# Row maxima of an attention kernel: turned through TensorE and ScalarE, or by VectorE's 32x32 exchange

## The chip, the cores and the metric

The kernel runs on one core of a Trainium2 chip. The metric is the device time of one execution in microseconds, lower being better. The median of three runs of the kernel before is 1864.71 us (1864.58 to 1864.8).

## What is computed

Two attention blocks over the same shapes (one batch, sequence S = 2048, width D = 640, 32 heads of width 20) are computed and their outputs are put side by side. Block A looks at a window of 8 keys with a dilation of 2. Block B is full attention, and the change lies in it:

```python
qkv = (x @ wqkv).reshape(B, S, 3, H, Dh).transpose(2, 0, 3, 1, 4)
q, k, v = qkv[0], qkv[1], qkv[2]
scores = jnp.einsum("bhqd,bhkd->bhqk", q, k) * (Dh ** -0.5)
p = _softmax(scores, axis=-1)
o = jnp.einsum("bhqk,bhkd->bhqd", p, v)
return o.transpose(0, 2, 1, 3).reshape(B, S, D) @ wo
```

All is in float32.

## The kernel before

**Stages.** First come the projections of A (queries, keys and values written to DRAM as rows), then the queries and keys of B (lines 492 to 529), then the values of B (lines 730 to 761), and then the main loop over B's attention (lines 791 to 836), with a short end that projects the last outputs. Block A's windowed attention is done almost wholly by GpSimd, a unit of work at a time (`a_attention`, lines 370 to 393), beside the main loop and the stages just ahead of it.

**Tiling of B.** The 32 heads are taken in 8 groups of 4, the 2048 queries in 4 blocks of 512. One group with one block of queries is a unit `u`; there are 32. A unit has 16 steps of 128 keys each, so the main loop has 512 steps. Step `i` does four things:

- `b_qk(i)`, lines 644 to 661: TensorE multiplies 128 keys by 512 queries for the 4 heads (62 contracted rows for each), into banks of PSUM called `ps_st`, and ScalarE takes the exponential into `e`.
- `b_pv(i - 2)`, lines 663 to 687: TensorE multiplies the exponentials by the values. Every second step ScalarE copies the sum out (`braw`, `more`) and GpSimd adds it up (line 683).
- `b_max(i + 24)`, lines 584 to 605: TensorE multiplies queries by keys once more with queries on the partitions (60 contracted rows), into the double tiles `ps_mx`, of which there are two. VectorE reduces each of them (128x1024 to 128x2) to the largest score, two reductions in a step. They are written into `m4`, which the profile shows as `mx`.
- pieces of other work: output groups, loads, GpSimd's units of block A.

For units 27 to 29, `b_both` (lines 607 to 639) does the first and the third of these in another order.

**What the change touches.** The largest score of every query is subtracted inside the score product itself: a query tile `bq` has two rows (60 and 61 of its 62) that hold the largest score as a sum of a high and a low part, and the matching rows of the key tile hold -1. The maxima are found with queries on partitions but have to lie along a row. `max_rows` (lines 535 to 555) does this once for each unit, 32 times in all:

- VectorE reduces `m4` to `m1`, 128 partitions by 16 (two halves of the contracted rows by two heads by four blocks of 128 queries).
- `turn` (lines 540 to 547) takes a bank of `ps_st`. TensorE turns `m1` into it (16x128), ScalarE copies it as float32r into `mt[:, 0]` (the high part; `mt` is `mtr` in the profile), VectorE subtracts that from the bank and writes the low part into `mt[:, 1]`, and the bank is given back.
- one step later SyncE's queue writes `mt` to DRAM, `md` (`mdr` in the profile), as 32 runs of 512 bytes.
- another step later `load` (lines 549 to 552) reads two pieces of `md` into the rows of `bq`.

**What sets the order.** The order of each engine's work is written out by hand. Every engine takes its instructions in the order of the program (`InOrder`, lines 48 to 56). `after(n, f)` runs `f` at the n-th next `tick()`, and the main loop ticks once at the head of a step. `b_max` of the last step of unit u runs in loop step 16u - 9; `odd(1)` puts the reduction to `m1` into step 16u - 7. `turn` is put on the list `rows` at the head of step 16u - 5, and it is taken off that list in the same step (line 821) just behind the first pair of score products; in units 29 to 31, whose maxima come from `b_both`, behind all of `b_both` (line 808). In the values' stage it is taken off at lines 756 and 757. The transfer to `md` is issued in step 16u - 4, the two loads in step 16u - 3, and the first score product that reads them is in step 16u.

Banks: `bank()` hands out four tiles `ps_st` in turn (lines 88 to 100), so that each use of one waits for the use four places before.

Of the kernel before, what the change touches and what calls it, by code (L numbers as in the profile page):

```python
# [8 lines left out]
F32 = mybir.dt.float32  # L9
F32R = mybir.dt.float32r  # L10
AF = mybir.ActivationFunctionType
ALU = mybir.AluOpType
# [47 lines left out]
def attention_pair(ctx, tc, xa, wqk_a, wv_a, wo_a, xb, wqk_b, wv_b, wo_b, oa, ob):  # L60
# [3 lines left out]
    sb = ctx.enter_context(tc.tile_pool(name="sb", bufs=1))  # L64
    ps = ctx.enter_context(tc.tile_pool(name="ps", bufs=1, space=PS))
    dr = ctx.enter_context(tc.tile_pool(name="dr", bufs=1, space=bass.MemoryType.DRAM))
    pe, dve, act, gp, sp = (InOrder(tc, e) for e in (nc.tensor, nc.vector, nc.scalar, nc.gpsimd, nc.sync))
# [5 lines left out]
    def after(n, fn, *args):  # L73
        due.setdefault(now[0] + n, []).append((fn, args))
# [3 lines left out]
    def odd(n):  # L78

        return n if loop[0] is None else n + (now[0] + n - loop[0] + 1) % 2  # L80

    def tick():
        now[0] += 1
        for fn, args in due.pop(now[0], ()):
            fn(*args)
# [5 lines left out]
    def bank():  # L91

        n = free.pop(0)
        t = ps.tile([128, 512], F32, tag=f"st{n}", bufs=1, name="ps_st")
        taken[id(t)] = (n, t)
        return t

    def give(t):

        free.append(taken.pop(id(t))[0])  # L100
# [45 lines left out]
    def chunk(t, xi, k):  # L146
        return t[k // (KC - 1)][:, xi, k % (KC - 1)]

    def x_pieces(x, n, second=None):

        t = columns(n)
        src = x[:, n * 512:(n + 1) * 512].rearrange("(k p) c -> p k c", p=128)

        def piece(a, b):
            u = t[a // (KC - 1)]
            m = a % (KC - 1)
            split(u[:, 0, m:m + b - a], u[:, 1, m:m + b - a], src[:, a:b], "p", second)
        return t, [lambda a=a, b=b: piece(a, b) for a, b in PAIRS]
# [58 lines left out]
    def rows15(p, o, W):  # L217

        for k in range(KC):
            for i, (wi, xi) in enumerate(PASSES):  # L220
                pe.matmul(p[:, :320], o(xi, k), W[wi][:, k], start=(k == 0 and i == 0), stop=(k == KC - 1 and i == 2))
# [40 lines left out]
    t, more = x_pieces(xa, 1)  # L262
# [6 lines left out]
    for n in (2, 3):  # L269
        t, more = x_pieces(xa, n)  # L270
        XA.append(t)
        loads += more
    ident = const.tile([128, 128], F32, name="ident")
# [149 lines left out]
    for n in range(NA):  # L423
        nxt = None
        for t in range(NT):
            if n == 0 and t < 4:
                p = first[t]
            else:
                p = next(banks)
# [51 lines left out]
    def v_piece(g, b0, b1):  # L481

        sp.dma_start(stacks[g][2][:, b0:b1], vb_d[b0 * 128:b1 * 128, g * GH * VC:g * GH * VC + VG]
                     .rearrange("(b p) c -> p b c", p=128))
# [8 lines left out]
    for m in range(0, 10, 2):  # L493
        nxt = []
        for n in range(4):
            for j in range(2):
                p = next(banks)
# [4 lines left out]
                c = MS[m + j]  # L502
# [27 lines left out]
    tick()  # L530


    rows = []

    def max_rows(m4, m1, q, qc):

        mt = sb.tile([16, 2, 128], F32R, tag="mtr", bufs=2, name="mtr")
        md = dr.tile([2, GH * 512], F32, tag="mdr", bufs=4, name="mdr")

        def turn():  # L540
            p = bank()
            pe.transpose(p[:16, :128], m1, ident)
            act.copy(mt[:, 0], p[:16, :128])
            dve.tensor_tensor(mt[:, 1], p[:16, :128], mt[:, 0].bitcast(F32), ALU.subtract)
            give(p)
            after(1, sp.dma_start, md.rearrange("t (j c) -> j t c", c=128), mt.bitcast(F32))
            after(2, load)

        def load():
            for r in range(2):  # L550
                sp.dma_start(q[r * HALF + BS:r * HALF + BM, qc].bitcast(F32),
                             md[:, r * 1024:(r + 1) * 1024].rearrange("t (p c) -> t p c", p=2))
        t = odd(1)
        after(t, dve.tensor_reduce, m1, m4.rearrange("p r a c -> p (r a) c"), AX.X, ALU.max)
        after(t + 2, rows.append, turn)

    def normalize(raw, g, c0, t, then):

# [25 lines left out]
    def b_max(i):  # L584

        u, sub = divmod(i, NKB)
        g, qc = divmod(u, NQC)
        q, k, v = stacks[g]
        if sub == 0:
            mxt[u] = (sb.tile([128, 2, 8, 4], F32, tag="mx4", bufs=2, name="mx4"),  # L590
                      sb.tile([128, 16], F32, tag="mx1", bufs=2, name="mx1"))
        m4, m1 = mxt[u]
        pq, ch = divmod(sub, 2)
        pl, qb = divmod(pq, 4)
        for c in (2 * ch, 2 * ch + 1):
            p = wide()
            for r in range(2):
                rows = slice(r * HALF, r * HALF + BS)
                pe.matmul(p[:, r], q[rows, qc, pl, qb * 128:qb * 128 + 128],
                          k[rows, pl, c * 512:(c + 1) * 512], start=True, stop=True)  # L600
            dve.tensor_reduce(m4[:, :, pq, c], p, AX.X, ALU.max)
            if c % 2 == 0:
                yield
        if sub == NKB - 1:
            max_rows(m4, m1, q, qc)

    def b_both(i):
# [30 lines left out]
        if sub == NKB - 1:  # L638
            max_rows(m4, m1, q1, qc1)
# [90 lines left out]
    for n in (2, 3, 0, 1):  # L730
        for half in range(2):
            for s in range(4 * n, 4 * n + 4):
                p = bank()
                rows15(p, lambda xi, k: chunk(XB[n], xi, k)[:, s % 4 * 128:s % 4 * 128 + 128], WV[half])
                ve = ones[s % 4]
                act.copy(ve[:, :16 * VC].rearrange("p (h c) -> p h c", c=VC)[:, :, :DH],
                         p[:, :320].rearrange("p (h d) -> p h d", d=DH))
                give(p)
                c = 16 * VC + 11 * half
                after(1, sp.dma_start, vb_d[s * 128:(s + 1) * 128, half * 16 * VC:half * 16 * VC + c], ve[:, :c])  # L740
                tick()
                groups += 1
                if q_loads:
                    for _ in range(4):
                        q_loads.pop(0)()
                if groups == 1:
                    wait[0] = 5
                if groups in (8, 16):
                    XB[groups // 8 - 1], more = x_pieces(xb, groups // 8 - 1, gp)
                    for fn in more:  # L750
                        fn()
                if groups > 8:
                    for i in islice(steps, 1):
                        for _ in b_max(i):
                            pass
                    if rows:
                        rows.pop(0)()
                if groups > 16 and groups % 3 == 0 and groups != 21:
                    next(a_work, None)
                if groups in (26, 28):  # L760
                    v_piece(0, *((0, 4) if groups == 26 else (8, 16)))
# [29 lines left out]
    for i in range(NS + LAG):  # L791
        g, sub = divmod(i, NQC * NKB)
        if sub == 16 and g + 1 < NG:
            k_loads, q_loads = b_pieces(g + 1)
            for n, fn in enumerate(k_loads + q_loads + [lambda g=g + 1: v_piece(g, 0, NKB)]):
                after(1 + n, fn)
        if i in (NS - 56, NS - 40):
            out_first((i - NS + 56) // NKB)
        tick()
        if loads and i % 2:  # L800
            loads.pop(0)()
        if i % 14 in (1, 5, 7, 11) and next(a_work, 0) == 0:
            for d in done_a:
                d[0] -= 1
        if i // NKB in ALONE and i + LEAD < NS:
            b_both(i)
            if rows and i % 2:
                rows.pop(0)()
            b_pv(i - LAG)
            if fill and i % 2 == 0:  # L810
                fill.pop(0)()
            elif i % 6 == 4 and not out_piece() and len(UNITS) == next_a[0] and not WO_b:
                for h in range(2):
                    w, more = wide_pieces(wo_b[h], gp)
                    WO_b.append(w)
                    loads += more
            continue
        qk = b_qk(i) if i < NS else iter(())
        next(qk, None)
        if rows and i % 2:  # L820
            rows.pop(0)()
        if i + LEAD >= NS:
            next(qk, None)
        if i >= LAG:
            b_pv(i - LAG)
        next(qk, None)
        mx = b_max(i + LEAD) if i + LEAD < NS else iter(())
        next(mx, None)
        if fill and i % 2 == 0:
            fill.pop(0)()  # L830
        elif i % 6 == 4 and not out_piece() and len(UNITS) == next_a[0] and not WO_b:
            for h in range(2):
                w, more = wide_pieces(wo_b[h], gp)
                WO_b.append(w)
                loads += more
        next(mx, None)
# [57 lines left out]
```

## Time and profile before

| | us |
|---|---|
| median of three runs | 1864.71 |
| the profiled execution, device time | 1864.39 |
| its span, first to last instruction | 1862.2 |
| busy: TensorE | 1818.1 |
| busy: ScalarE | 1374.9 |
| busy: VectorE | 1321.9 |
| busy: GpSimd | 1198.5 |

The profile is one execution, taken by the hardware profiler. PE is TensorE, PEld its loading of weights, DVE VectorE, ACT ScalarE, POOL GpSimd and SP SyncE, whose queue issues the transfers. All the program's instructions are issued by one helper, so that every row carries line 56, and a group is told by its tiles: output, an arrow, inputs. In a group's row stand the count, the busy time in us with the mean of one in ns, and behind the bar the idle time of the engine just before, with what ended it. In a row of the timeline stand the start and the length in us, the engine, the instruction, the tiles, the shapes, how many were merged, and in brackets the idle time ahead of it. The granted clock of TensorE was 0.998 over the span.

### The profile page before, as it was taken

The page shows a single profiled execution, that of the slowest core. Times are in us where ns is not written, and L with a number is a line of the kernel's source. Part 1 is how long each engine was busy: PE and PEld are TensorE (multiplying, and loading weights), DVE is VectorE, ACT ScalarE, POOL GpSimd, SP SyncE. Part 2 cuts the span into 40 slices and gives each one's busy share as a digit, 9 for nine tenths or more (in the row PEclk, how much of TensorE's full clock was granted, in tenths as well). Part 3 has the DMA queues.
Part 4 walks back from the last instruction along what each step waited for, and adds up shares of the span by engine and source line. Part 5 has one row for each costly group of instructions (what it writes and reads, how often), then busy time and mean ns, then how long its engine had stood idle before and what let it go on. Part 6 is the DMA issues. An engine that isn't in the chain of part 4 may idle for free.

```text
span 1862.2 us, 30622 instructions
## 1 busy us (share of the span) xinstructions
PE 1818.1 (98%) x11323; PEld 977.7 (52%) x11323; DVE 1321.9 (71%) x1286; ACT 1374.9 (74%) x2669; POOL 1198.5 (64%) x998
## 2 busy tenths in 40 slices
PE   9999999999999999999999999999999999999999
PEld 8888888885443433434434334343343344333558
DVE  3000332278889899898898998989989989999400
ACT  4222322224889899898898998989989988999882
POOL 0000075048989898898888988989889762557232
PEclk9999999999999999999999999999999999999999
DMA  6333686755542254345234432642452332111023
GB/s 222 113 95 115 206 291 234 229 156 172 135 132 95 96 158 141 97 113 153 89 103 133 137 98 89 165 137 75 129 162 86 99 75 61 54 31 49 29 67 111
DMA packets 144110, 229.74 MB, mean 123 GB/s; under 512 B 43100, under 2 KB 74460, under 8 KB 142968
## 3 DMA queue, kind: packets, MB, share of 16 engines
q1 hardware_dynamic: 143384, 227.13, 39.7%
q8 instruction: 89, 1.46, 0.3%
q10 hardware_dynamic: 576, 0.66, 0.1%
q14 instruction: 61, 0.50, 0.1%
HBM read 168.05 MB, written 59.67 MB: 122 GB/s over the span
## 4 chain that ended last, share of the span: by engine, by line
PE 64%; DVE 26%; ACT 6%; issue 2%; POOL 1%; POOLq 0%; ACTq 0%
PE ps_st L56 45%; DVE mx L56 25%; PE ps_mx L56 20%; ACT e L56 4%; ACT more L56 1%; POOL akv L56 1%; DVE am L56 0%; POOL braw L56 0%; DVE aot L56 0%; ACT aot L56 0%; POOL ao L56 0%; DVE sm L56 0%; ACT braw L56 0%; POOL am L56 0%; ACT ro L56 0%
## 5 line engine op out<-in xcount | busy, mean ns | idle before, releaser
L56 DVE TENSOR_REDUCE mx<-ps_mx 128x2 f32<-128x1024 f32 x1024 | 1201.3, 1221 | 143.6 <-PE ps_mx L56 136.8
L56 ACT ACTIVATE e<-ps_st 128x512 f32<-128x512 f32 x2000 | 1063.8, 615 | 50.9 <-PE ps_st L56 23.1
L56 PE MATMUL ps_st<-e,vb 128*32 128x512 f32 x4096 | 546.4, 606 | 1.0 <-ACT e L56 0.6
L56 PE MATMUL ps_st<-bq,bk 62*128 62x512 f32 x2000 | 491.2, 453 | 0.3
L56 PEld LDWEIGHTS ps_st<-bq,bk 62*128 62x128 f32 x2000 | 256.5, 184 | 439.0 <-ACT e L56 406.9
L56 POOL TENSOR_TENSOR braw<-braw,more 128x512 f32<-128x512 f32 x248 | 318.9, 1286 | 250.6 <-ACT more L56 247.8
L56 PE MATMUL ps_mx<-bk,bq 60*128 60x512 f32 x2048 | 442.7, 443 | 32.5 <-DVE mx L56 18.2
L56 POOL TENSOR_TENSOR akv<-akv,aq 128x1280 f32<-128x1280 f32 x64 | 188.3, 2943 | 236.7 <-DMA akv<-ka_d 236.7
L56 PEld LDWEIGHTS ps_mx<-bk,bq 60*128 60x128 f32 x2048 | 205.2, 185 | 180.8 <-DVE mx L56 168.5
L56 POOL TENSOR_TENSOR akv<-akv 128x640 f32<-128x640 f32 (+3 forms) x304 | 281.8, 927 | 23.8
L56 ACT COPY ro<-ps_st 128x320 f32<-128x320 f32 (+1 forms) x92 | 43.6, 474 | 159.3 <-PE ps_st L56 114.5
L56 PEld LDWEIGHTS ps_st<-e,vb 128*32 128x32 f32 x4096 | 80.9, 108 | 151.5 <-ACT e L56 87.0
L56 ACT COPY more<-ps_st 128x512 f32<-128x512 f32 x248 | 149.6, 603 | 11.6 <-PE ps_st L56 5.4
L56 POOL TENSOR_TENSOR akv<-akv,al 128x1280 f32<-128x1280 f32 x64 | 151.4, 2366 | 0.2
L56 PE MATMUL ps_st<-ww,xn 128*128 128x320 f32 x720 | 120.0, 315 | 0.2 <-ACT braw L56 0.2
L56 PEld LDWEIGHTS ps_st<-ww,xn 128*128 128x128 f32 x720 | 106.7, 188 | 20.8 <-ACT more L56 7.5
L56 POOL TENSOR_TENSOR xn<-stg,xn 128x512 fp32r<-128x512 f32 (+1 forms) x20 | 30.1, 1507 | 92.4 <-ACT xn L56 91.1
L56 DVE TENSOR_TENSOR wc<-stg,wc 128x480 fp32r<-128x480 f32 (+5 forms) x15 | 8.4, 559 | 101.6 <-ACT wc L56 101.5
L56 PE MATMUL ps_st<-ww,aot 128*128 128x320 f32 x480 | 78.8, 316 | 0.0
L56 POOL TENSOR_TENSOR ao<-ao,akv 128x640 f32<-128x640 f32 x48 | 74.8, 1558 | 3.8
L56 PEld LDWEIGHTS ps_st<-ww,aot 128*128 128x128 f32 x480 | 70.4, 188 | 11.3 <-ACT e L56 10.6
L56 ACT COPY ro<-ps_mx 128x480 f32<-128x480 f32 x32 | 18.0, 562 | 72.4 <-PE ps_mx L56 62.8
(85 smaller groups left out, 1290.1 us busy)
## 6 DMA issues: line engine op xcount, KB each, us to landing
akv<-ka_d SPq DMA_DIRECT2D x128, 320.0 KB
akv<-va_d SPq DMA_DIRECT2D x128, 320.0 KB
kb_d<-pr SPq DMA_DIRECT2D x20, 512.0 KB
qb_d<-pr SPq DMA_DIRECT2D x20, 512.0 KB
bk<-kb_d SPq DMA_DIRECT2D x16, 640.0 KB
bq<-qb_d SPq DMA_DIRECT2D x64, 160.0 KB
rb<-s_d SPq DMA_DIRECT2D x128, 64.0 KB
stg<-xb SPq DMA_DIRECT2D x12, 512.0 KB
```

The lines of the kernel that those rows point to most:

```text
L56: return lambda *a, **k: self.tc.keep_in_program_order(op(*a, **k))
```

## The change

The maxima are turned by VectorE alone. `mt` becomes 128 partitions by 2 by 32. VectorE copies `m1` as float32r into the first 16 columns of `mt[:, 0]` (the high part), subtracts it from `m1` into the other 16 (the low part), and exchanges rows and columns within each block of 32 partitions by 32 columns, from `mt[:, 0]` into `mt[:, 1]`. Each partition then holds 32 successive queries of one of the 32 rows, and the transfer to `md` gathers the four blocks: 128 runs of 128 bytes instead of 32 runs of 512. The two loads from `md` stay. The bank of PSUM, the product on TensorE and the copy on ScalarE go. The list `rows` goes too, so that `turn` runs at the head of its step.

```diff
-    rows = []
 
     def max_rows(m4, m1, q, qc):
 
-        mt = sb.tile([16, 2, 128], F32R, tag="mtr", bufs=2, name="mtr")
+        mt = sb.tile([128, 2, 32], F32R, tag="mtr", bufs=2, name="mtr")
         md = dr.tile([2, GH * 512], F32, tag="mdr", bufs=4, name="mdr")
 
         def turn():
-            p = bank()
-            pe.transpose(p[:16, :128], m1, ident)
-            act.copy(mt[:, 0], p[:16, :128])
-            dve.tensor_tensor(mt[:, 1], p[:16, :128], mt[:, 0].bitcast(F32), ALU.subtract)
-            give(p)
-            after(1, sp.dma_start, md.rearrange("t (j c) -> j t c", c=128), mt.bitcast(F32))
+
+            dve.tensor_copy(mt[:, 0, :16], m1)
+            dve.tensor_tensor(mt[:, 0, 16:], m1, mt[:, 0, :16].bitcast(F32), ALU.subtract)
+            dve.transpose(mt[:, 1].bitcast(F32), mt[:, 0].bitcast(F32))
+            after(1, sp.dma_start, md.rearrange("t (j b c) -> b (t j) c", b=4, c=32), mt[:, 1].bitcast(F32))
             after(2, load)
...
-        after(t + 2, rows.append, turn)
+        after(t + 2, turn)
...
-                    if rows:
-                        rows.pop(0)()
...
-            if rows and i % 2:
-                rows.pop(0)()
...
-        if rows and i % 2:
-            rows.pop(0)()
```

## The prediction, made before the result was known

> **What bounds the kernel now.** I read the page first, then the engines by stretches, then VectorE's timeline over a few steps.
>
> ```profile
> span 1862.2 us, 30622 instructions
> PE 1818.1 (98%) x11323; PEld 977.7 (52%) x11323; DVE 1321.9 (71%) x1286; ACT 1374.9 (74%) x2669; POOL 1198.5 (64%) x998
> PE 64%; DVE 26%; ACT 6%; issue 2%; POOL 1%; POOLq 0%; ACTq 0%
> ```
>
> ```profile
> 900.00:1000.00 100.00, 97.00 (x651) 40.80 (x649) 89.93 (x85) 90.35 (x177) 90.08 (x79) 1.00 0.32 100
> ```
>
> The chain that ended last runs over TensorE and VectorE. The row of 100 us from the main loop gives busy time of PE, PEld, DVE, ACT and POOL in this order: 97 for TensorE and, PEld aside, three times about 90. So nothing is far from being the bound, and an added microsecond is judged from the steps around it. VectorE's rows:
>
> ```profile
> 927.78 4.67 DVE L56 TENSOR_REDUCE mx<-ps_mx 128x2 f32<-128x1024 f32 x4 [0.68 <-PE ps_mx L56]
> 932.70 4.68 DVE L56 TENSOR_REDUCE mx<-ps_mx 128x2 f32<-128x1024 f32 x4 [0.24 <-PE ps_mx L56]
> 937.30 0.62 DVE L56 TENSOR_REDUCE am<-al 128x32 f32<-128x256 f32 x1
> 937.82 4.61 DVE L56 TENSOR_REDUCE mx<-ps_mx 128x2 f32<-128x1024 f32 x4
> 942.35 0.25 DVE L56 RECIPROCAL sm<-sm 128x16 f32<-128x16 f32 x1
> 942.51 0.17 DVE L56 TENSOR_REDUCE mx<-mx 128x16 f32<-128x64 f32 x1
> 942.67 4.69 DVE L56 TENSOR_REDUCE mx<-ps_mx 128x2 f32<-128x1024 f32 x4
> 947.27 0.27 DVE L56 TENSOR_TENSOR mtr<-ps_st,mtr 16x128 fp32r<-16x128 f32 x1
> 947.87 4.62 DVE L56 TENSOR_REDUCE mx<-ps_mx 128x2 f32<-128x1024 f32 x4 [0.33 <-PE ps_mx L56]
> 952.74 4.68 DVE L56 TENSOR_REDUCE mx<-ps_mx 128x2 f32<-128x1024 f32 x4 [0.24 <-PE ps_mx L56]
> ```
>
> Four reductions are two steps. From start to start a pair of steps takes 4.92 us (927.78 to 932.70), 5.12, 4.85, 5.20 and 4.87. 4.87 to 4.92 is the plain pair, with VectorE idle for 0.24 us until TensorE delivers: TensorE bounds it by a hair. The pair with the reduction `am` (0.62 us, which puts off the next start by 0.52, since a start overlaps the end before it) takes 0.2 us more, while the two small instructions at 942.35, which put it off by 0.32, cost nothing. So **VectorE has some 0.32 us of cover in a pair, and what it does beyond that is paid in full**: both tiles of `ps_mx` are then full and TensorE stands before the next one, with all that is queued behind:
>
> ```profile
> PEld ps_mx L56 <- DVE mx L56: 169.5, 393, 1.2
> ```
>
> The pair with the turn (942.67 to 947.87) is the one of 5.20.
>
> **What goes.** The groups by shape:
>
> ```profile
> L56 DVE TENSOR_TENSOR xn<-stg,xn 128x1024 fp32r<-128x1024 f32 x14 | 17.2, 1226 | 33.6 <-ACT xn L56 33.5
> ...
> L56 PE MATMUL ps_st<-ident,mx 128*16 128x128 f32 x32 | 8.9, 277 | 0.1
> L56 DVE TENSOR_TENSOR mtr<-ps_st,mtr 16x128 fp32r<-16x128 f32 x32 | 8.6, 270 | 10.7 <-ACT mtr L56 10.7
> L56 ACT CAST mtr<-ps_st 16x128 fp32r<-16x128 f32 x32 | 7.7, 240 | 0.4 <-PE ps_st L56 0.4
> L56 DVE RECIPROCAL sm<-sm 128x16 f32<-128x16 f32 x32 | 7.8, 243 | 5.8 <-DMA sm<-s_d 5.8
> L56 DVE TENSOR_REDUCE mx<-mx 128x16 f32<-128x64 f32 x32 | 5.4, 168 | 0.1
> ...
> L56 DVE TENSOR_TENSOR xn<-stg,xn 128x512 fp32r<-128x512 f32 x4 | 2.8, 693 | 0.5 <-ACT xn L56 0.3
> ```
>
> A turn costs TensorE 0.28, ScalarE 0.24 and VectorE 0.27 us. They do not add up. VectorE's lies inside the cover, for 0.33 us of idleness follow it. TensorE's does not: 5.20 less 4.92, the longer of the plain pairs, is 0.28 us, the product itself. Times 32: **-9.0 us**. ScalarE's copy and the bank held over it are in that difference already. What is late next, when the product goes, is VectorE.
>
> **What comes, if nothing disturbs it.** The change adds three VectorE instructions, each needing the one before. 512 and 1024 elements take 693 and 1226 ns, so a subtraction takes about 160 ns and 1.04 ns for each element: 177 ns for 16, and 193 for an exchange of 32, taken as costing the same. The copy lies between the 168 of the small reduction and that 177. No row shows an exchange or a VectorE copy from SBUF to SBUF; the bounds for either are 0.16 us (the small reduction at 942.51, from its start to the next one's) and 0.25 (the reciprocal at 942.35, the slowest row of this width), and I take the low end, since neither computes as a reciprocal does. Two hand-overs of about 0.03 to 0.08 us come in between (GpSimd starts one 0.07 us behind the end of the one that it needs, at 264.43 below). Sum 0.17 + 0.03 + 0.18 + 0.03 + 0.19 = 0.60 us, which is the `am` reduction's 0.62, and so about 0.20 us beyond the cover in each of the 32 turns: **+6.4 us** (nothing, if the `am` pair's 0.2 us came from something else in it; 14 with both instructions at 0.25 and both hand-overs at 0.08, 0.84 in all). These two parts alone would give -2.6 us.
>
> **What comes on top: a wait on GpSimd.** Before, the subtraction read PSUM and SBUF. Now both its inputs are in SBUF. Where that happens while GpSimd works, the trace shows what follows. VectorE's and GpSimd's rows from the stage of B's queries and keys:
>
> ```profile
> 263.67 1.37 DVE L56 TENSOR_TENSOR w<-stg,w 128x640 fp32r<-128x640 f32 x1
> ...
> 294.42 1.21 DVE L56 TENSOR_TENSOR w<-stg,w 128x640 fp32r<-128x640 f32 x1
> ```
>
> ```profile
> 261.39 2.97 POOL L56 TENSOR_TENSOR akv<-akv,aq 128x1280 f32<-128x1280 f32 x1
> 264.43 2.03 POOL L56 TENSOR_TENSOR akv<-akv 128x640 f32<-128x640 f32 x1
> ...
> 291.99 2.96 POOL L56 TENSOR_TENSOR akv<-akv,aq 128x1280 f32<-128x1280 f32 x1
> ```
>
> ```profile
> L56 DVE TENSOR_TENSOR w<-stg,w x10: 825/826/1370, 180.0 to 321.8; 128x640 fp32r<-128x640 f32 x10
> ```
>
> The subtraction of 128x640 takes 825 ns, but 1.37 us when it starts with 0.69 us left of a GpSimd instruction, and 1.21 when 0.53 are left. **It waits for the end of GpSimd's instruction less 0.15 us.** The price here follows from what GpSimd does at the turns. I went through all 32, with the old subtraction's start as the moment; first and last of those with a wait, VectorE's and GpSimd's rows, and GpSimd's at the turn quoted above:
>
> ```profile
> 517.90 0.27 DVE L56 TENSOR_TENSOR mtr<-ps_st,mtr 16x128 fp32r<-16x128 f32 x1
> ...
> 1712.22 0.27 DVE L56 TENSOR_TENSOR mtr<-ps_st,mtr 16x128 fp32r<-16x128 f32 x1
> ```
>
> ```profile
> 517.80 1.29 POOL L56 TENSOR_TENSOR braw<-braw,more 128x512 f32<-128x512 f32 x1
> ...
> 947.18 1.56 POOL L56 TENSOR_TENSOR akv<-akv 128x640 f32<-128x640 f32 x1
> ...
> 1712.12 1.30 POOL L56 TENSOR_TENSOR braw<-braw,more 128x512 f32<-128x512 f32 x1
> ```
>
> At 517.90, 1.19 us are left of GpSimd's instruction; at 947.27, 1.47; at 1712.22, 1.20. Fifteen turns have 0.2 us or more left, 14.2 us together, so 12.0 of waiting. The new subtraction comes 0.2 us later, behind the copy: 3.0 less. But in about seven other turns GpSimd is just ending or about to start an instruction of 1.28 or 1.56 us, as those rows last, and the later subtraction runs into it, for some 1.2 us each: 8.4 more. Sum 17.4 us, and all of it lies beyond the cover, which the chain has used up: **+17.4 us**. The exchange waits behind the subtraction, the four reductions of the next pair behind the exchange, and TensorE behind those.
>
> A one-input instruction need not wait: the reciprocals `sm`, main loop or not, keep to their time:
>
> ```profile
> L56 DVE RECIPROCAL sm<-sm x32: 240/242/254, 513.1 to 1827.5; 128x16 f32<-128x16 f32 x32
> ```
>
> So I cost the copy and the exchange without a wait. For the exchange no page speaks against that. For the copy one does: the Trainium skill (page "SBUF — State Buffer", section "Who interferes with whom") has it that copies and casts may run in a mode that takes both of VectorE's ports, and that such an instruction and one of GpSimd's shut each other out for their whole length. No run here shows such a copy. By the rows the sum is +14.8; by that page the copy would wait as well, which is the second rival, with up to +38.8.
>
> **The transfer.** 128 runs of 128 bytes replace 32 of 512. The nearest is the write of `sm` in 128 runs of 64 bytes. SyncE's queue, and the first score product after the loads:
>
> ```profile
> 942.62 0.32 SPq L56 DMA_DIRECT2D s_d<-sm  x1
> 944.03 1.72 SPq L56 DMA_DIRECT2D rb<-s_d  x4
> ...
> 947.57 0.33 SPq L56 DMA_DIRECT2D mdr<-mtr  x1
> 950.90 0.54 SPq L56 DMA_DIRECT2D bq<-mdr  x2
> ```
>
> ```profile
> 957.81 0.40 PE L56 MATMUL ps_st<-bq,bk 62*128 62x512 f32 x2
> ```
>
> The read behind that write of short runs is issued 1.41 us after it, so it had landed by then; here 3.33 us lie between the write and the load, and 6.4 between the load's issue and its use. The transfer costs nothing: its issue keeps its step, one instruction for one, and only what SyncE holds behind the load (GpSimd's `akv`) could come later. If its cover were gone, each turn would pay what exceeds it.
>
> Moving `turn` to the head of its step leaves it between the same reductions of VectorE, except in units 29 to 31, where it goes ahead of two: nothing, since the maxima are used five steps later.
>
> **The sum.** -9.0 + 6.4 + 17.4 = +14.8 us. Against the profiled execution's 1864.39 us (span 1862.2, and 2.2 around it) that is 1879.2, against the median of the runs, 0.3 higher, 1879.5: I say **1880**.
>
> **The rivals.**
>
> *No wait: not slower.* The same three instructions fall into GpSimd's gaps. For it: 17 of the 32 turns have under 0.2 us of a GpSimd instruction left, and GpSimd's additions to `braw` start when ScalarE has copied, so their place shifts when the product goes. It decides once fewer than 3 turns wait, at about a microsecond each. Against it: GpSimd is busy 90 us in 100. Price -2.6 us: 1862; with the chain's cost at its lower bound, nothing, -9.0: 1856. Chance 0.18.
>
> *Two waits in a turn.* The copy waits for GpSimd's instruction, and while it runs the next one queues; the subtraction, which needs the copy's result, finds that one at work. By the 15 turns with a wait, 12.0 us; and in these and the six where the next instruction follows at once, a whole one of 1.28 to 1.56 us: 21 by 1.4 = 29.4. With -2.6: +38.8, 1903 (1885 where the subtraction sometimes slips in first). For it: GpSimd pauses only 0.07 us between its instructions. Against it: no row shows a one-input instruction that waits. The page named above would have it so. Chance 0.28.
>
> *The transfer comes late.* If short runs landed over 6 us later, the first product of a unit would wait and each microsecond would cost 32; 1900 at one. Chance 0.03.
>
> **How the numbers follow.** One wait in a turn has 0.46, two 0.28, none 0.18, the transfer 0.03, and 0.05 is for what I do not see (0.02 faster, 0.01 the same, 0.02 slower). Under 0.2% (3.7 us) a measurement of this kernel tells little from no change. Half of "no wait" is faster by more, half within. So faster 0.11, same 0.10, slower 0.79. The range goes from the price of no wait, 1862, to just over that of two, 1905; about 0.1 lies outside at either end.
>
> **What would show it.** The product `ps_st<-ident,mx` and ScalarE's `mtr` are gone. The subtraction `mtr<-mx,mtr` has a minimum near 180 ns and, in about 20 of 32, some 0.2 to 1.5 us more, ending with a GpSimd instruction. If the copy shows such lengths as well, it is the second rival; if neither does, the first. Turn pairs take 5.1 us undisturbed, and up to 6.5 with a wait. The load from `mdr` still goes out 5 us or more ahead of its use. The forecast is wrong if VectorE's wait exists and TensorE does not stand for it, or if the exchange takes much over 0.34 us.

## The result, and the profile after

The changed kernel takes 1894.51 us (median of 5 runs, 1888.42 to 1899.93) against 1864.71: a ratio of 1.0164, 95% interval 1.0153 to 1.0175. It is slower by 29.8 us; 15 were forecast.

Its page, in the order of the rows shown of the kernel before:

```profile
span 1886.5 us, 30518 instructions
PE 1816.0 (96%) x11291; PEld 970.6 (51%) x11291; DVE 1356.0 (72%) x1350; ACT 1371.4 (73%) x2637; POOL 1198.0 (64%) x998
...
PE 64%; DVE 32%; issue 1%; DMA 1%; ACT 0%; SPq 0%; POOL 0%; POOLq 0%; ACTq 0%
```

VectorE is busy for 34.1 us more with 64 instructions more, and its share of the chain that ended last went from 26% to 32%. The groups by shape and the tile `mtr` (shortest, middle and longest in ns) tell which instructions:

```profile
L56 DVE CAST mtr<-mx 128x16 fp32r<-128x16 f32 x32 | 25.8, 806 | 0.0
L56 DVE TENSOR_TENSOR mtr<-mx,mtr 128x16 fp32r<-128x16 f32 x32 | 14.0, 438 | 1.1
L56 DVE STREAM_TRANSPOSE mtr<-mtr 128x32 f32<-128x32 f32 x32 | 6.8, 212 | 1.1
```

```profile
L56 DVE CAST mtr<-mx x32: 161/814/1881, 426.1 to 1773.2; 128x16 fp32r<-128x16 f32 x32
L56 DVE TENSOR_TENSOR mtr<-mx,mtr x32: 174/176/2844, 427.5 to 1773.4; 128x16 fp32r<-128x16 f32 x32
L56 DVE STREAM_TRANSPOSE mtr<-mtr x32: 211/212/215, 428.0 to 1773.7; 128x32 f32<-128x32 f32 x32
```

Undisturbed, the three take 0.16, 0.17 and 0.21 us. The exchange always does. The subtraction does in most turns. The copy, a one-input instruction which I had costed without a wait, has a middle of 0.81. Above their undisturbed time the copies hold 25.8 - 32 x 0.165 = 20.5 us and the subtractions 14.0 - 32 x 0.175 = 8.4.

VectorE's rows of two turns, and GpSimd's beside them:

```profile
648.65 1.51 DVE L56 CAST mtr<-mx 128x16 fp32r<-128x16 f32 x1
650.20 0.17 DVE L56 TENSOR_TENSOR mtr<-mx,mtr 128x16 fp32r<-128x16 f32 x1
650.41 0.21 DVE L56 STREAM_TRANSPOSE mtr<-mtr 128x32 f32<-128x32 f32 x1
...
1301.56 0.60 DVE L56 CAST mtr<-mx 128x16 fp32r<-128x16 f32 x1
1302.20 2.84 DVE L56 TENSOR_TENSOR mtr<-mx,mtr 128x16 fp32r<-128x16 f32 x1
```

```profile
648.57 1.56 POOL L56 TENSOR_TENSOR akv<-akv 128x640 f32<-128x640 f32 x1
650.21 1.57 POOL L56 TENSOR_TENSOR ao<-ao,akv 128x640 f32<-128x640 f32 x1
...
1300.84 1.29 POOL L56 TENSOR_TENSOR braw<-braw,more 128x512 f32<-128x512 f32 x1
1302.09 2.92 POOL L56 TENSOR_TENSOR akv<-akv,aq 128x1280 f32<-128x1280 f32 x1
```

Read the ends. GpSimd's instruction of 648.57 ends at 650.13 and the copy at 650.16. The subtraction starts at 650.20, GpSimd's next at 650.21: it slips in by a hundredth of a microsecond and takes its 0.17 us. At 1301.56 the copy again ends with GpSimd's instruction (1302.13), but GpSimd's next had started at 1302.09, ahead of the end of the one before, and the subtraction stands through nearly the whole of it: 2.84 us. So it is throughout: the copies of 22 turns and the subtractions of 8 waited, and each of these 30 ends 0.03 to 0.04 us behind the end of an instruction of GpSimd.

TensorE pays, as the waits show (in all, times, longest). Before, the first row read 169.5 us with a longest of 1.2, and the second:

```profile
PE ps_mx L56 <- DVE mx L56: 22.5, 85, 0.7
```

After:

```profile
PEld ps_mx L56 <- DVE mx L56: 208.7, 438, 2.9
...
PE ps_mx L56 <- DVE mx L56: 50.8, 118, 2.6
```

### The profile page after: what moved, and what is told of

Its sections match the earlier page's. It is cut to its first block, busy times and chain, and to the rows that moved or that the text cites. A ratio compares the mean times of both kernels' runs of the same rounds, so it can differ in the third digit from the quotient of the medians.

```text
span 1886.5 us, 30518 instructions
## 1 busy us (share of the span) xinstructions
PE 1816.0 (96%) x11291; PEld 970.6 (51%) x11291; DVE 1356.0 (72%) x1350; ACT 1371.4 (73%) x2637; POOL 1198.0 (64%) x998
## 4 chain that ended last, share of the span: by engine, by line
PE 64%; DVE 32%; issue 1%; DMA 1%; ACT 0%; SPq 0%; POOL 0%; POOLq 0%; ACTq 0%
PE ps_st L56 44%; DVE mx L56 29%; PE ps_mx L56 20%; DVE mtr L56 2%; DMA rb<-s_d 1%; DVE am L56 0%; ACT aot L56 0%; DVE aot L56 0%; DMA s_d<-sm 0%; DMA bq<-qb_d 0%; DVE sm L56 0%; SPq L56 0%; POOL braw L56 0%; ACT e L56 0%; ACT braw L56 0%
## 5 line engine op out<-in xcount | busy, mean ns | idle before, releaser
L56 PEld LDWEIGHTS ps_st<-bq,bk 62*128 62x128 f32 x2000 | 251.2, 184 | 434.9 <-ACT e L56 421.0
L56 DVE TENSOR_TENSOR xl<-stg,xl 128x512 fp32r<-128x512 f32 x12 | 8.3, 688 | 95.6 <-ACT xl L56 95.6
```

Source lines behind the costliest of these rows:

```text
L56: return lambda *a, **k: self.tc.keep_in_program_order(op(*a, **k))
```

## The experiments

Two theories stood against each other. **S**: the copy and the subtraction both wait for GpSimd's instruction, and what VectorE loses beyond its cover is paid. **C**: the chain of three dependent instructions itself is too long for its place. **T** put the cost on the transfer or on the turn's new place in its step. Each ratio is to the kernel before, run beside on the same chip.

**e1: the copy as a reduction.** The same values, but an instruction of another kind:

```diff
-            dve.tensor_copy(mt[:, 0, :16], m1)
+            dve.tensor_reduce(mt[:, 0, :16], m1.unsqueeze(2), AX.X, ALU.max)
```

> The copy of the changed kernel is written as a maximum over an axis of length one: the same values, one input, but an instruction of the reduction's kind. Theory S (VectorE's copy and its two-input subtraction both wait for GpSimd's instruction, and what VectorE loses beyond some 0.3 us of cover in a pair of steps is paid in full): this copy takes about 0.17 us in all 32 turns, the subtraction behind it meets GpSimd in about 20 turns and waits 15 to 20 us in all; time 12 to 20 us over before, 1877 to 1885. Rival C (three dependent instructions on VectorE are too long a chain at that place, whatever they are): as the changed kernel, 1888 to 1900. Rival T (the transfer with short runs, or the place of the turn at the head of its step): also 1888 to 1900.

Measured: 1877.27 us, ratio 1.0067 (1.0053 to 1.0080). This is the kernel that I had forecast, one in which the subtraction alone waits, and it is slower by 12.0 us. A turn, VectorE's rows and GpSimd's:

```profile
650.72 0.16 DVE L56 TENSOR_REDUCE mtr<-mx 128x16 fp32r<-128x16 f32 x1
650.91 1.34 DVE L56 TENSOR_TENSOR mtr<-mx,mtr 128x16 fp32r<-128x16 f32 x1
652.28 0.21 DVE L56 STREAM_TRANSPOSE mtr<-mtr 128x32 f32<-128x32 f32 x1
```

```profile
650.65 1.57 POOL L56 TENSOR_TENSOR akv<-akv 128x640 f32<-128x640 f32 x1
```

The reduction runs through while GpSimd is at work; the subtraction behind it ends with GpSimd's instruction. Its group takes 22.6 us, 17.0 of them waiting, in 23 turns:

```profile
L56 DVE TENSOR_TENSOR mtr<-mx,mtr x32: 174/628/1668, 426.2 to 1763.0; 128x16 fp32r<-128x16 f32 x32
```

**e2: the subtraction replaced.** It is left out; the low part is the high part again:

```diff
-            dve.tensor_tensor(mt[:, 0, 16:], m1, mt[:, 0, :16].bitcast(F32), ALU.subtract)
+            dve.tensor_reduce(mt[:, 0, 16:], mt[:, 0, :16].bitcast(F32).unsqueeze(2), AX.X, ALU.max)
```

> The subtraction of the changed kernel is replaced by a maximum over an axis of length one that reads only the high part. It leaves out the subtraction: the low part is then the high part again. Theory S: the copy still waits in about 20 turns, 20 us in all, the replaced instruction takes 0.17 us always; time 13 to 20 us over before, 1878 to 1885. If only two-input instructions waited, as my forecast had it: no wait at all, 1860 to 1866. Rivals C and T: 1888 to 1900.

Measured: 1884.81 us, ratio 1.0110 (1.0096 to 1.0124). Its copies:

```profile
L56 DVE CAST mtr<-mx x32: 165/816/1898, 425.9 to 1770.2; 128x16 fp32r<-128x16 f32 x32
```

The copy alone waits, in 23 turns, and it costs more than the subtraction alone. "Only two-input instructions wait" has fallen.

**e3: both replacements.** 

> Both replacements at once (the subtraction is left out, the low part is the high part again). Theory S: three instructions of 0.17, 0.17 and 0.21 us in every turn and no wait; by the forecast's terms, -9.0 for the turn through TensorE and +6.4 for the chain, 1862, between 1859 and 1866. Rivals C and T: the time of the changed kernel, 1888 to 1900.

Measured: 1862.73 us, ratio 0.9983 (0.9973 to 0.9992). The tile `mtr` of e3:

```profile
L56 DVE TENSOR_REDUCE mtr<-mx x32: 158/159/170, 425.9 to 1747.8; 128x16 fp32r<-128x16 f32 x32
L56 DVE TENSOR_REDUCE mtr<-mtr x32: 169/170/172, 426.1 to 1748.0; 128x16 fp32r<-128x16 f32 x32
L56 DVE STREAM_TRANSPOSE mtr<-mtr x32: 211/211/214, 426.3 to 1748.2; 128x32 f32<-128x32 f32 x32
```

The chain is as long as in the undisturbed turns of the changed kernel, the transfer and the place are its own, and the whole loss is gone with the waits, with GpSimd at work as before: 22 of the 32 first reductions lie wholly inside one of its instructions. C and T have fallen. TensorE's wait `PE ps_mx <- DVE mx`, 50.8 us in the changed kernel, is 42.3 us in e2, 37.8 in e1 and 27.8 here, in the order of the times.

**e4: no turn at all**, from the kernel before. The turn is left out and the rows come from a tile of zeros, so that no maximum is subtracted:

```diff
-            p = bank()
-            pe.transpose(p[:16, :128], m1, ident)
-            act.copy(mt[:, 0], p[:16, :128])
-            dve.tensor_tensor(mt[:, 1], p[:16, :128], mt[:, 0].bitcast(F32), ALU.subtract)
-            give(p)
-            after(1, sp.dma_start, md.rearrange("t (j c) -> j t c", c=128), mt.bitcast(F32))
+            after(1, sp.dma_start, md.rearrange("t (j c) -> j t c", c=128), flat)
```

> The kernel before without the turn: no product on TensorE, no copy on ScalarE, no subtraction on VectorE; the rows come from a tile of zeros, so that no maximum is subtracted. The transfers stay. It gives what any other way of turning can gain. By the forecast's term of 0.28 us in 32 turns, -9.0: 1855.7. If the turn were hidden before: 1864.7. If ScalarE's copy and the bank count as well (0.28 + 0.24 + 0.27 in 32 turns): 1840.

Measured: 1857.22 us, ratio 0.9959 (0.9947 to 0.9972), 8.1 us under the runs beside it (1865.28). That is what a turn through TensorE cost, and so about the most that any other way can gain by taking its place.

**e5: the kernel before with its turn at the head of the step:** `after(t + 2, turn)` in place of the list.

> The kernel before with the turn at the head of its step, as the change has it, through TensorE and ScalarE still. If the place in the step costs nothing (my forecast): 1862 to 1868. If it matters, because TensorE then asks for the turn ahead of the score products that would have kept it busy: up to 0.5 us in 32 turns, 1868 to 1881, and part of the change's cost would be this and not the waits.

Measured: 1875.81 us, ratio 1.0061 (1.0048 to 1.0073). The place was forecast at nothing, and for a turn through TensorE it counts for 11.2 us. The wait that grew is TensorE's for VectorE's `mtr`, the last user of the turn's bank, from 2.1 us in all to 30.6, while its wait for ScalarE's `mtr` fell from 15.9 to 0.9; why the place does this was not tested:

```profile
PEld ps_st L56 <- DVE mtr L56: 30.6, 30, 1.4
```

For the changed kernel it does not count, as e3 has the same place.

**e6 and e7: what a microsecond of VectorE costs at that place.** From e3, with n useless reductions of SBUF ahead of the exchange, 2 in e6 and 7 in e7:

```diff
+            for _ in range(2):
+                dve.tensor_reduce(idle, mask, AX.X, ALU.max)
             dve.transpose(mt[:, 1].bitcast(F32), mt[:, 0].bitcast(F32))
```

> The kernel with both replacements (no wait on GpSimd, low part left out as there) and two more reductions of 128x256 in SBUF on VectorE in every turn, ahead of the exchange, of no use: some 0.3 to 0.4 us each, so 0.6 to 0.8 in a turn. Theory S: the chain has used the cover up, so all of it is paid, 32 times 0.6 to 0.8 over 1862.7, 1882 to 1888, with some loss of clock on top. If VectorE has more slack around the turns than I hold, below 1873.

Measured: 1879.86 us, ratio 1.0085 (1.0071 to 1.0099), just under the 1882 to 1888 expected and 17.1 over e3: 0.54 us a turn, of some 0.66 added. (e3 ran on another chip; with each set against the kernel before on its own chip the difference is 17.8.) So most of what comes on top of the chain is paid, a little less than I held.

> As the kernel with both replacements (low part left out as there), with seven useless reductions of 128x256 in a turn instead of two (0.41 us each in the trace, some 0.33 from start to start). Two of them cost 17.1 us in 32 turns, 0.54 in each. If only VectorE's time counts: seven cost 3.5 times that, 60 to 75 us, 1923 to 1938, at a granted clock of 0.997 or 0.998 as before. If TensorE's standing still for 2 us and more is followed by a stretch at half clock, as one such stretch of 3.4 us follows a wait of 2.8 us in the trace of the changed kernel: a granted clock of 0.96 to 0.99, and the time 10 to 50 us higher than that.

Measured: 2007.82 us, ratio 1.0768 (1.0750 to 1.0786), which is 145 us over e3, about twice the 60 to 75 us expected of VectorE's time alone, and above the 1988 us at which the expectation's other branch ends. The cores' view of e7, and its stretches around a turn (busy PE, PEld, DVE, ACT and POOL, then the granted clock):

```profile
core 0: 2004.1 us, clock 0.961
```

```profile
1040.00:1049.50 9.50, 7.55 (x51) 4.21 (x51) 7.66 (x15) 6.48 (x13) 8.95 (x10) 1.00 0.36 115
1049.50:1056.30 6.80, 6.28 (x26) 2.06 (x28) 4.73 (x5) 3.50 (x7) 5.05 (x7) 0.50 0.60 173
1056.30:1090.00 33.70, 32.88 (x223) 13.63 (x215) 30.13 (x29) 29.94 (x59) 23.63 (x15) 1.00 0.59 152
```

After a turn in which TensorE stood for about 2 us, its clock is halved for 6.8 us. The trace has 30 such stands of 1.9 us or more, and 28 of them are followed by a stretch at half clock, of 3.4 or 6.8 us. A clock of 0.961 over 2004 us means 78 us of TensorE's time lost; if all of it is paid, this execution (2006.0 us) would stand at 1928 without it, inside the 1923 to 1938 expected of VectorE's time alone. The expectation had the kind of cost right and put it too low, at 10 to 50 us.

**e10: the changed kernel again.** 

> The changed kernel once more, for its spread and its granted clock on the chip of the other runs of this call. Its five runs went from 1888.4 at a clock of 0.999 to 1899.9 at 0.992. If the clock makes the spread: the same range again, and the longer of the profiled runs at the lower clock.

Measured: 1900.22 us (1898.98 to 1904.66), ratio 1.0190 (1.0175 to 1.0205), from the upper end of the first range to a little above it. The cores' view of its profile, and of the first profile of the changed kernel:

```profile
core 0: 1898.3 us, clock 0.991
```

```profile
core 0: 1886.5 us, clock 0.999
```

The waits are nearly the same in both (copies 26.3 us against 25.8 in all, subtractions 15.1 against 14.0), the clock is not: 17.1 us of TensorE's time lost here (0.009 of 1898), 1.9 there. The difference, 15.2, is more than the 11.8 between the spans. All nine runs say the same: their spans go from 1886.5 to 1902.8 us, and less the time lost, from 1881 to 1886. So the spread of the changed kernel's runs is the clock's.

The trace of e10 has eight stretches at half clock ahead of its last 2 us. One, of 6.8 us from 446.0, lies at the start of the main loop and stands in the kernel before as well (from 445.4). The other seven, of 3.4 us each, all start 5 to 7 us behind the start of a copy that waited, and TensorE stood for 0.7 to 2.6 us in between. The first of the seven, with what lies ahead of it:

```profile
479.40:483.60 4.20, 1.79 (x12) 0.64 (x14) 4.17 (x5) 1.53 (x4) 4.04 (x5) 1.00 0.19 69
483.60:487.00 3.40, 3.40 (x20) 1.24 (x16) 2.03 (x3) 2.55 (x5) 1.86 (x3) 0.50 0.81 275
```

So most of the lost clock comes behind the same waits: they leave TensorE standing, and some of these stands are followed by a stretch at half clock. Which ones are followed differs from run to run; of that I show no cause.

**e8: copy and subtraction out of PSUM.** The whole computation; the maxima are reduced into the tile of PSUM that VectorE has just read:

```diff
+        m1 = p[:, 0, :16]
+        dve.tensor_reduce(m1, m4.rearrange("p r a c -> p (r a) c"), AX.X, ALU.max)
+        dve.tensor_copy(mt[:, 0, :16], m1)
+        dve.tensor_tensor(mt[:, 0, 16:], m1, mt[:, 0, :16].bitcast(F32), ALU.subtract)
+        dve.transpose(mt[:, 1].bitcast(F32), mt[:, 0].bitcast(F32))
+        t = odd(1) + 3
...
-        after(t, dve.tensor_reduce, m1, m4.rearrange("p r a c -> p (r a) c"), AX.X, ALU.max)
-        after(t + 2, turn)
```

> The whole computation. The reduction to the maxima writes into the tile of PSUM that VectorE has just reduced (16 columns of it), so that the copy and the subtraction read PSUM and the subtraction has one input in SBUF; all four instructions follow the last reduction of a unit at once, some four steps earlier than in the change, and the transfers keep their steps. Theory S: nothing waits for GpSimd, copy 0.16 to 0.2 us, subtraction 0.17 to 0.2; time that of both replacements, 1859 to 1866. If the wait comes from GpSimd being at work at all, whatever VectorE reads: 1888 to 1900. If holding the tile of PSUM costs TensorE its next product: 5 to 15 us over 1863.

Measured: 1875.41 us, ratio 1.0063 (1.0049 to 1.0076). Its tile `mtr`, and TensorE's wait for it:

```profile
L56 DVE CAST mtr<-ps_mx x32: 174/174/176, 420.8 to 1761.7; 128x16 fp32r<-128x16 f32 x32
L56 DVE TENSOR_TENSOR mtr<-ps_mx,mtr x32: 174/174/175, 421.0 to 1761.9; 128x16 fp32r<-128x16 f32 x32
```

```profile
PE ps_mx L56 <- DVE mtr L56: 21.5, 25, 1.1
```

No copy and no subtraction waits for GpSimd any more, though 16 of the copies and 22 of the subtractions lie wholly inside an instruction of GpSimd: it is the operands in SBUF that make them wait. The gain is lost again, for TensorE now waits 25 times, 0.9 us each, for the tile that the chain holds: the expectation's third branch.

**e9: the high part alone.** The reduction writes float32r into a tile whose other half stays zero, `dve.tensor_reduce(mt[:, 0, :16], m4...)`, with no copy; the low part is left out.

> The reduction writes the high part itself, as float32r, into a tile whose other half stays zero, and the exchange follows in the turn. It leaves out the low part: what is subtracted from a query's scores is then the maximum to the precision of float32r, the same for all its keys. VectorE's part of a turn is the exchange alone, 0.21 us, inside the cover. Theory S: all of the gain that leaving the turn out gave, 1856 to 1859, and clear of the kernel before. If the exchange's 0.21 us is paid in full: 1863 to 1865.

Measured: 1857.78 us, ratio 0.9962 (0.9949 to 0.9974). That is the gain of e4 (0.9959): the exchange alone fits into the cover.

**e11: the subtraction on GpSimd.** The whole computation, and GpSimd itself does what would have to wait for it:

```diff
-            dve.tensor_copy(mt[:, 0, :16], m1)
-            dve.tensor_tensor(mt[:, 0, 16:], m1, mt[:, 0, :16].bitcast(F32), ALU.subtract)
...
+        for out in (m1, mt[:, 0, :16]):
+            after(t, dve.tensor_reduce, out, m4.rearrange("p r a c -> p (r a) c"), AX.X, ALU.max)
+        after(t, pool, mt[:, 0, 16:], m1, mt[:, 0, :16].bitcast(F32), ALU.subtract)
```

> The whole computation. VectorE reduces twice, once to the maxima and once to the high part as float32r; GpSimd subtracts (128x16, some 0.2 to 0.3 us on its own queue) in the same step, and VectorE's exchange follows two steps later. No instruction of VectorE has two inputs in SBUF or copies within it. Theory S: VectorE has 0.16 and 0.21 us in two different pairs of steps, both inside the cover, so nearly all of the gain of leaving the turn out: 1856 to 1861. If GpSimd comes to its subtraction more than 5 us late, the exchange waits for it and all of VectorE with it: each microsecond in 32 turns is 32 us, 1866 to 1900.

Measured: 1854.65 us, ratio 0.9952 (0.9938 to 0.9965): it beats both kernels. It lies a little under the 1856 to 1861 expected and gains 9.5 us where e4 gained 8.1; the two intervals overlap, and its runs had clocks of 0.999 and 1.0 where e4's had 0.997 to 0.999, so no further gain is shown. Its tile `mtr`:

```profile
L56 POOL TENSOR_TENSOR mtr<-mx,mtr x32: 214/222/232, 422.3 to 1741.9; 128x16 fp32r<-128x16 f32 x32
L56 DVE STREAM_TRANSPOSE mtr<-mtr x32: 199/202/211, 426.6 to 1742.1; 128x32 f32<-128x32 f32 x32
```

GpSimd subtracts in 0.22 us, VectorE waits for it 0.3 us in all of the span, and the exchange's 0.20 us lies in another pair of steps than the second reduction. GpSimd pays instead: it stands for 69.2 us in all until VectorE has reduced, which costs nothing here, for the time is no longer than e4's.

## Why the prediction was right in direction and wrong in size

- **The turn through TensorE, forecast -9.0 us.** Measured -8.1 (e4).
- **The chain undisturbed, forecast +6.4.** Measured 1862.73 - 1857.22 = +5.5 (e3 over e4; the place and the short runs of the transfer are in it). Both together give -2.5, with -2.6 forecast.
- **The subtraction's wait, forecast +17.4.** Where it is the only one that waits, 1877.27 - 1862.73 = +14.5 (e1 over e3), of 17.0 us of waiting in the trace. The rule read off two rows of an early stage, that VectorE waits for the end of GpSimd's instruction, carried over to instructions of 16 elements. The count behind the 17.4 did not hold, and that it came out so near is luck. In the trace of the kernel before, 19 turns, not 15, have 0.2 us or more of a GpSimd instruction left, 20.9 us together and not 14.2, and the first of them is at 428.87, not 517.90. But only two turns, not seven, would run into GpSimd's next instruction 0.2 us later. By the prediction's own rule these moments 0.2 us later give 17 turns and 18.1 us: the two errors cancel. The first of the 19:

```profile
428.87 0.27 DVE L56 TENSOR_TENSOR mtr<-ps_st,mtr 16x128 fp32r<-16x128 f32 x1
```

```profile
428.84 2.94 POOL L56 TENSOR_TENSOR akv<-akv,aq 128x1280 f32<-128x1280 f32 x1
```

- **The step that failed: "a one-input instruction need not wait ... so I cost the copy and the exchange without a wait."** It holds for the exchange and not for the copy. The row that it leaned on, the reciprocals', was of another kind of instruction. The copy was put at 0.17 us in every turn; it took 0.81 in the mean. Its wait costs 1884.81 - 1862.73 = +22.1 us alone (e2 over e3), and with the subtraction's 31.8. They do not add up to 36.6: behind a copy that has waited, the subtraction mostly slips in before GpSimd's next.
- **The page that I weighed and gave the smaller chance was right.** The Trainium skill (page "SBUF — State Buffer", section "Who interferes with whom") has it that copies and casts can be shut out by GpSimd, which the copies' 0.16 to 1.88 us here show; reductions, by the same section, never are, and e3's never were (0.16 to 0.17).
- **The second rival, "two waits in a turn"**, had the mechanism, and its price of 1903, or 1885 where the subtraction slips in, holds the result between its ends; for the 1885 it shows no working. Its account is not the measured one: the copy waits in 22 turns, not 15, and the subtraction in 8, not 21. The 15 were miscounted, as said, and taken in the old schedule; the moments shift with the change.
- **Not foreseen: the clock.** In the profile at a clock of 0.999 the change costs 24 us (1888.42 against 1864.39); the four other runs lie 5.7 to 11.5 us above that one, at clocks of 0.992 to 0.996. So of the 29.8 us some 24 are the terms above, with the copy's wait, and some 6 are time lost to the clock, a term that the prediction did not have. The 24 fit: -2.5, and most of the 29 us that copies and subtractions wait in that trace.
- **The transfer, forecast at nothing,** costs nothing: e3 has it. In the changed kernel's trace the loads go out 5.3 us or more ahead of the first product that needs them, as before.
- **The cover** of some 0.32 us in a pair of steps, what is beyond it paid: borne out by e9, e11 (inside it, free) and e6 (beyond it, four fifths paid).

## What to carry to other kernels

Before work is moved to VectorE, ask where each operand lies and of what kind the instruction is: beside a busy GpSimd, a copy or a two-input subtraction within SBUF of 16 elements costs up to a whole GpSimd instruction, while a reduction and the 32x32 exchange do not. A copy can be written as a reduction over an axis of one, or be folded into the reduction before it, and a small two-input operation can go to GpSimd itself, if its result is wanted some steps later and GpSimd is not the bound. A row that shows one kind of instruction not waiting is no evidence for another kind.

## What the runs showed of the hardware

The exchange of a 128x32 tile of float32 took 0.20 to 0.22 us in every kernel, whatever GpSimd did. VectorE's dependent instructions follow each other by 0.03 to 0.04 us (650.16 to 650.20 above), GpSimd's by 0.07 to 0.08. TensorE's clock was halved for 6.8 us after a stand of about 2 us in e7, and in the changed kernel for 3.4 us after its longest stand, 2.56 us; that stretch and the one ahead of it (PE, PEld, DVE, ACT and POOL busy, then the granted clock, third number from the right):

```profile
1300.00:1306.40 6.40, 3.89 (x28) 1.18 (x26) 6.33 (x7) 4.87 (x10) 6.16 (x6) 1.00 0.43 136
1306.40:1309.80 3.40, 3.35 (x12) 2.91 (x13) 2.26 (x2) 0.00 (x0) 3.09 (x6) 0.50 0.05 12
```
